# A linear-attention and gated feed-forward kernel: rows of x in another tile's place, loads and stores of x at other times, and another order of some splits

## The chip, the core and the metric

The kernel runs on one core of a Trainium2 chip. Its time is the device time of one execution in microseconds (us); the smaller, the better. The core has TensorE (PE; its weight loads are listed as PEld), VectorE (DVE), ScalarE (ACT), GpSimd (POOL) and SyncE (SP), which here issues every DMA.

## What is computed

For x of 2048 rows and 576 columns, in float32:

```
xn  = layernorm(x)
q,k,v = xn @ wqkv              (32 heads of 18 columns)
pq, pk = phi(q), phi(k)        phi(t) = (t > 0 ? t + 1 : exp(t)) + 1e-6
kv, z = sum over rows of pk v, sum over rows of pk      (per head)
s   = (pq kv) / (pq z + 1e-6) @ wo
g   = silu( gelu(xn @ w1 + b1) @ w2 + b2 )              (576 -> 4608 -> 576)
out = x + s * g
```

## The kernel before

Every float32 product is made of three: an operand is written as a rounded part `h` and a remainder `l`, both in the type fp32r, and TensorE adds h·h, h·l and l·h in PSUM. Making the two is a *split*: a copy to fp32r (`hi`, mostly on ScalarE, line 656) and a subtraction (`lo`, mostly on VectorE, line 659). SBUF tiles of xn, transposed, are `xh0`..`xh3` (five tiles of 128 rows by 512 columns each; 576 = 4·128 + 64, and the last 64 rows stand twice, once as `h` and once as `l`) and `xl0`..`xl3` (four each), one pair for every 512 rows of x, in the pool `xp`.

**Phase 1** (to about 166 us) runs over 16 tiles of 128 rows of x. Tile t loads x (`load_x`), takes mean and variance (`layernorm`, line 175 on), normalises, transposes on TensorE into PSUM (`transpose_x`, line 206), copies to `xh` and subtracts for `xl`, multiplies by the weights of k and v (`project`, line 229: 14 matmul pairs into one PSUM tile) and adds up the state. The loads run ahead: x of tile t+3 is issued in tile t. Each weight of k is five pieces, `wk_h` and `wk_l`, split at the start. Along the way other things are prepared: W2's sums (`w2r`), the last rows of w1 (`we`), the splits of wq (loaded in tiles 11 to 13), and xh0, xl0 and parts of xh1, xl1 are written to the DRAM tensor `x_dram` (after tiles 4 and 8), since their places are used for other things and the second half of the feed-forward needs them again.

All DMAs are in SP's one queue, in program order; a DMA on SP also waits for the one eight before it.

**The query phase** (to about 285 us) finishes the attention. It also makes the operands that the feed-forward's seven-product scheme wants: sums of blocks of x, and the last 64 rows of each of the seven products (`rest`), split and written to `rq_dram`.

**The feed-forward** (300 to 1082 us) treats the rows of x in two halves, and each half in nine chunks of 512 hidden columns, 18 chunks in all; a tail follows the last, whose down product is a plain one. So 17 chunks are alike. A chunk has 28 steps. Steps 0 to 13 are two `Up` objects: each makes a 2 by 2 block product with seven products instead of eight, in the order 1, 6, 7, 5, 2, 3, 4 (`Up.step`). Its PSUM tiles are `a`, `b`, `e` and `zy`; three intermediate sums, `m1`, `u1`, `u2`, stand in SBUF, in the tile `mid`. VectorE makes `b<-e,mid` (line 996), `e<-e,mid` (1003) and `zy<-zy,mid` (1007), and ScalarE makes a gelu `g` of each result (978). The products take xh, xl and the `rest` tile `rx` of their number as moving operands (`mm`). Steps 14 to 27 are the seven down products (`product`, line 1100) in the order 1, 2, 7, 4, 5, 3, 6, each in two calls (two of four quarters of 128 rows at a time). Product 2 adds to what product 1 left in its PSUM tile, 3 to that of 5 and 4 to that of 7 (`CHAIN`); before that, VectorE adds the tile of 1, 5 or 7 into the accumulator `macc` (line 1107), and TensorE waits for this.

The operands of the down products are the gelu results and their sums: POOL makes the sums in place, `S` (5,.) at line 1060, (6,.) at 1063, (3,.) at 1066 and (7,.) at 1069, where (i, pr) is the product and which of the two `Up`s. Each operand is split by `hi` (ScalarE, 656) and `lo` (VectorE, 659). At which step of the chunk each of them is put in program order is written out by hand in the table `PH`, and `in_order` holds VectorE, ScalarE, POOL and TensorE to the program's order. The lines of `PH` for `lo` are

```
            (1, 0): 10, (2, 0): 10, (7, 0): 11, (1, 1): 12, (2, 1): 13, (7, 1): 15, (4, 0): 16,
            (4, 1): 17, (5, 1): 18, (5, 0): 19, (6, 0): 20, (3, 0): 21, (3, 1): 22, (6, 1): 23,
```

Step 11 is the one in which the second `Up` makes its product 2, 12 is its product 3 (`e`), 13 its product 4 (`zy`). So VectorE's order at the end of the second `Up` is lo(1,0), lo(2,0), lo(7,0), e, lo(1,1), zy, lo(2,1), macc of product 1, ...

Memory: `mid` has the place of `xh1` in the pool `xp` (five tiles of 128 by 512; three for m1, u1, u2 and two for the operands of product 7). The rows `rest` of the products 5, 2, 3, 4 have four tiles of 128 by 512 in the pool `rx`, loaded by `load_rests` from `rq_dram`, two DMAs each; those of the other products are loaded elsewhere.

Of the kernel before, what the change touches and what calls it, by code (L numbers as in the profile page):

```python
# [8 lines left out]
F32 = mybir.dt.float32  # L9
# [6 lines left out]
P = 128  # L16
# [6 lines left out]
NT = S // P  # L23
# [19 lines left out]
def linear_attention_gated_ffn(ctx, tc, x, wqkv, wo, w1, w1e, b1, w2, b2, out):  # L43
# [121 lines left out]
    def load_x(t):  # L165
        xraw[t] = (
            stw.tile([P, D], F32, tag="stw", name=f"x{t}") if t < 2 else stage(D, f"x{t}")
        )
        nc.sync.dma_start(xraw[t], x[t * P : (t + 1) * P, :])

    xn, stats = {}, {}

    def layernorm(t):
        st = t1.tile([P, 2, 6], F32, tag="st", name=f"st{t}")
        nc.vector.bn_stats(st[:, 0, :], xraw[t][:, :HD])
        nc.vector.bn_stats(st[:, 1, :], xraw[t][:, HD:])
        mv = t1.tile([P, 4], F32, tag="mv", name=f"mv{t}")
        nc.vector.bn_aggr(mv[:, 0:2], st)
        nc.vector.tensor_scalar_add(mv[:, 2:3], mv[:, 1:2], 1e-5)
        nc.gpsimd.tensor_tensor(mv[:, 3:4], mv[:, 2:3], nhalf, op=ALU.pow)  # L180
        stats[t] = mv
        if t < 2:
            xn[t] = t1.tile([P, 640], F32, tag="xn", name=f"xn{t}")
            for dst, src in norm_parts(t):
                nc.vector.tensor_scalar(dst, src, mv[:, 0:1], mv[:, 3:4], op0=SUB, op1=MUL)
# [17 lines left out]
    def transpose_x(t):  # L203
        pt = bank2(f"pt{t}").rearrange("p a b -> p (a b)")
        for k in range(KT):
            nc.tensor.transpose(pt[:, k * P : (k + 1) * P], xn[t][:, k * P : (k + 1) * P], ident)  # L206
        b, c = divmod(t, 4)
        cs = slice(c * P, (c + 1) * P)
        p3 = pt[:, : KT * P].rearrange("p (k c) -> p k c", k=KT)
        if t == 0:  # L210
            nc.vector.tensor_copy(xh[b][:, :2, cs], p3[:, :2])
            nc.vector.tensor_copy(xh[b][:, 2:, cs], p3[:, 2:])
        else:
            nc.scalar.copy(xh[b][:, :, cs], p3)
        nc.vector.tensor_tensor(xl[b][:, :, cs], p3[:, :4, :], xh[b][:, :4, cs].bitcast(F32), op=SUB)
        nc.vector.tensor_tensor(
            xh[b][64:, 4, cs], p3[64:, 4, :], xh[b][64:, 4, cs].bitcast(F32), op=SUB
        )

    def project(t, hi, lo, ps):  # L220
        b, c = divmod(t, 4)
        cs = slice(c * P, (c + 1) * P)
        seq = []
        for k in range(4):
            seq += [(xh[b][:, k, cs], hi, k), (xh[b][:, k, cs], lo, k), (xl[b][:, k, cs], hi, k)]
        seq += [(xh[b][:, 4, cs], hi, 4), (xh[b][:, 4, cs], lo, 4)]
        for i, (st, w, k) in enumerate(seq):
            for h in range(2):
                nc.tensor.matmul(  # L229
                    ps[:, h, :HD], st, w[:, k, h * HD : (h + 1) * HD],  # L230
                    start=(i == 0), stop=(i == len(seq) - 1),
                )
# [11 lines left out]
    def load_w_raw(which, k):  # L244
# [4 lines left out]
        nc.sync.dma_start(raw, wqkv[k, :, which * D : (which + 1) * D])  # L249
        return raw  # L250

    def split_w(raw, k, hi, lo, elo):
        nc.scalar.copy(hi[:, k, :], raw)
        elo.tensor_tensor(lo[:, k, :], raw, hi[:, k, :].bitcast(F32), op=SUB)


    warm = bank1("warm")
# [158 lines left out]
    load_x(0)  # L416
    raw_k = [load_w_raw(1, k) for k in range(KT)]
    load_x(1)
    layernorm(0)
    split_w(raw_k[0], 0, wk_h, wk_l, nc.vector)  # L420
    split_w(raw_k[1], 1, wk_h, wk_l, nc.gpsimd)
    transpose_x(0)
    split_w(raw_k[2], 2, wk_h, wk_l, nc.gpsimd)
    split_w(raw_k[3], 3, wk_h, wk_l, nc.vector)
    split_w(raw_k[4], 4, wk_h, wk_l, nc.gpsimd)
    raw_v = [load_w_raw(2, k) for k in range(KT)]
    load_x(2)
    layernorm(1)
    pend = None
    WQ_LOADS = {11: (0,), 12: (1, 2), 13: (3, 4)}  # L430
    WQ_SPLITS = {13: (0,), 14: (1, 2), 15: (3, 4)}
    raw_q = {}
    for t in range(NT):
        if t + 3 < NT:
            load_x(t + 3)
        if t == 1:
            we_load(0), we_load(1)
        if 0 < t < NT - 2:
            layernorm(t + 2)
        pk = bank2(f"pk{t}")  # L440
        project(t, wk_h, wk_l, pk)
        if t == 0:
            for k in range(KT):
                split_w(raw_v[k], k, wv_h, wv_l, nc.vector)
        if t + 1 < NT:
            if t + 1 in (8, 12):
                x_block((t + 1) // 4)
            transpose_x(t + 1)
        for j in W2_SUMS.get(t - 1, ()):
            w2_hi(j)  # L450
        for j in W2_SUMS.get(t - 1, ()):
            w2_lo(j)
        if 2 <= t < 2 + WG:
            we_hi(t - 2), we_lo(t - 2)
        if t == 0:
            layernorm(2)
        if t + 2 < NT:
            offset(t + 2)
        k_t, _ = phi(t1, pk, f"k{t}")
        if pend is not None:  # L460
            state(*pend)
        pv = bank2(f"pv{t}")
        project(t, wv_h, wv_l, pv)
        v_t = t1.tile([P, D], F32, tag="v", name=f"v{t}")
        nc.scalar.copy(as2(v_t), pv[:, :, :HD])  # L465
        if t + 2 < NT:
            normalize_x(t + 2)
        if t == 0:
            nc.gpsimd.memset(zacc, 0.0)
        for j in W2_SUMS.get(t, ()):  # L470
            w2_sum(j)
        if 1 <= t < 1 + WG:
            we_sums(t - 1)
        nc.gpsimd.tensor_tensor(zacc, zacc, k_t, op=ADD)
        for k in WQ_SPLITS.get(t, ()):
            split_w(raw_q[k], k, wq_h, wq_l, nc.gpsimd if k == 0 else nc.vector)
        for k in WQ_LOADS.get(t, ()):
            raw_q[k] = load_w_raw(0, k)
        for j in W2_SUMS.get(t - 1, ()):
            w2_store(j)  # L480
        if 2 <= t < 2 + WG:
            we_store(t - 2)
            if t < WG:
                we_load(t)
        for c in W2_LOADS.get(t, ()):
            w2_load(c)
        if t == KT + 2:
            make_mask()
            nc.gpsimd.memset(kvz, 0.0)
        pend = (t, k_t, v_t)  # L490
        if t in (4, 8):
            b = t // 4 - 1
            if b == 0:
                nc.sync.dma_start(x_dram[:, 0:4], xh[0][:, :4].bitcast(F32))
                nc.sync.dma_start(x_dram[:, 4:8], xl[0].bitcast(F32))
            else:
                nc.sync.dma_start(x_dram[:, 10:12], xh[1][:, 2:4].bitcast(F32))
                nc.sync.dma_start(x_dram[:, 14:16], xl[1][:, 2:].bitcast(F32))
    nc.sync.dma_start(b1c, b1)
    query(0)  # L500
    state(*pend)
# [425 lines left out]


    gp = ctx.enter_context(tc.tile_pool(name="gp", bufs=1, side="right", reuse_waits="tile"))
    rx = ctx.enter_context(tc.tile_pool(name="rx", bufs=1, side="right", reuse_waits="tile"))  # L930
    gg = ctx.enter_context(tc.tile_pool(name="gg", bufs=NGT, side="right", reuse_waits="tile"))
    fr = ctx.enter_context(tc.tile_pool(name="fr", bufs=1, side="right", reuse_waits="tile"))
    fl = ctx.enter_context(tc.tile_pool(name="fl", bufs=1, reuse_waits="tile"))
# [4 lines left out]
    nc.sync.dma_start(b2b, bass.AP(tensor=b2.tensor, offset=b2.offset, ap=[[0, P], [1, D]]))  # L938
    BIAS = {2: 0, 7: 1, 3: 1, 4: 0}

    def load_rests(half, some):

        out = {}
        for i in some:
            out[i] = rx.tile([P, 512], F32R, tag=f"rx{i}", name=f"rx{i}")
            load_rest(half, i, out[i])
        return out

    mid = xp.tile([P, KT, 512], F32R, tag="xh1", name="mid").bitcast(F32)
    m1_sb, u1_sb, u2_sb = (mid[:, i, :] for i in range(3))  # L950

    class Up:

# [88 lines left out]
    class HOps:  # L1042
# [11 lines left out]
        def S(self, i, pr):  # L1054
            A = lambda r, c: self.A[pr, r, c]
            tt = nc.gpsimd.tensor_tensor
            src = self.src
            if i == 5:
                src[5, pr] = A(1, 0)
                tt(src[5, pr], A(1, 0), A(1, 1), op=ADD)  # L1060
            elif i == 6:
                src[6, pr] = A(0, 0)
                tt(src[6, pr], src[5, pr], A(0, 0), op=SUB)  # L1063
            elif i == 3:
                src[3, pr] = A(0, 1)
                tt(src[3, pr], A(0, 1), src[6, pr], op=SUB)  # L1066
            else:
                src[7, pr] = mid[:, 3 + pr, :]
                tt(src[7, pr], A(0, 0), A(1, 0), op=SUB)  # L1069

        def hi(self, i, pr):
# [202 lines left out]
    def plan_w1(add, w, base, T, hi, lo):  # L1274
        for table, what in ((T, w.T), (hi, w.hi), (lo, w.lo)):
# [23 lines left out]
            (4, 1): 17, (5, 1): 18, (5, 0): 19, (6, 0): 20, (3, 0): 21, (3, 1): 22, (6, 1): 23,  # L1299
        },  # L1300
        lo={
            (1, 0): 10, (2, 0): 10, (7, 0): 11, (1, 1): 12, (2, 1): 13, (7, 1): 15, (4, 0): 16,
            (4, 1): 17, (5, 1): 18, (5, 0): 19, (6, 0): 20, (3, 0): 21, (3, 1): 22, (6, 1): 23,
        },
    )
# [14 lines left out]
    w2t[0].load_raw()  # L1320
    z = xsum[1]
    s2, s1, s4 = z.tiles
    xs = x_operands(z.h0, z.l0, z.h1, z.l1, s1, s2, s4, load_rests(1, (5, 2, 3, 4)))
    seq = ExitStack()
    seq.enter_context(in_order(nc.vector.engine, nc.scalar.engine, nc.gpsimd.engine, nc.tensor.engine))
    n_chunks = 2 * NC
    for step in range(n_chunks):
# [36 lines left out]
        if not plain:  # L1364
            if half == 0 and c == NC - 1:
                for k, at in X_AT.items():
                    add(base + at, load_x_part, k)
                add(base + 14, lambda: x_new.update(rs=load_rests(0, (5, 2, 3, 4))))
                add(base + 25, silu_first, C11)
                for k in range(2):  # L1370
                    add(base + 26 + k, combine, C12, nc.vector, slice(2 * k, 2 * k + 2))
# [95 lines left out]
```

## Time and profile before

| | us |
|---|---|
| three runs | 1115.74, 1117.62, 1121.1 |
| median | 1117.62 |
| profiled execution, its own time | 1114.33 |
| its span, first to last instruction | 1112.6 |
| TensorE busy | 1100.2 |
| VectorE busy | 806.6 |
| POOL busy | 455.1 |
| ScalarE busy | 454.8 |

The granted clock of TensorE was 1.000 over the whole span. The profile is of one execution. A row of a timeline is: start in us from the span's start, duration, engine, line of the kernel, operation, the tile written and those read (names without their numbers), how many instructions lie in the row, and in brackets how long the engine was idle before it and for whom. A row of waits has the time lost, how often, and the longest. A row of the page's fifth part has the number of instructions, the busy time of all in us, and the mean in ns, then the idle time before them. A busy matmul engine is not necessarily one at its peak: the matmuls are pipelined, and a usual 288-column matmul of a down product follows the one before after 0.133 us.

### The profile page before, as it was taken

To read this page: it belongs to the slowest core of one execution; us is meant where nothing else is said; L and a number is where in the kernel's file an instruction comes from. 1 tells how busy PE (TensorE), PEld (TensorE's weight loads), DVE (VectorE), ACT (ScalarE), POOL (GpSimd) and SP (SyncE) were. 2 spreads that over 40 slices of the span, in tenths; PEclk is the share of its full clock that TensorE was granted. 3 is DMA by queue.
4 is the path that set the end of the run, shared out by engine and by line. 5 is a ranking of instruction groups with operands and counts; after the bars stand their busy time and mean duration, and the time that the engine had idled before them with its cause. 6 is when DMAs were issued, how large, how long until landed. Compare 5 with 4: busy or idle time off the path is not lost.

```text
span 1112.6 us, 18603 instructions
## 1 busy us (share of the span) xinstructions
PE 1100.2 (99%) x6972; PEld 1018.2 (92%) x6972; DVE 806.6 (72%) x1159; ACT 454.8 (41%) x771; POOL 455.1 (41%) x392
## 2 busy tenths in 40 slices
PE   8989999999999999999999999999999999999998
PEld 8989998999998988989989899898898998989987
DVE  7667547999687887878878878666485574764866
ACT  4544444333544354453543544524233242242342
POOL 4966533333353463444524534325234142241340
PEclk9999999999999999999999999999999999999999
DMA  8698642364879568586595779997777677776552
GB/s 316 254 367 325 246 155 52 117 248 165 262 273 342 178 235 293 196 301 218 184 348 179 257 264 356 323 348 253 244 247 220 199 239 216 237 219 213 136 182 85
DMA packets 84968, 264.03 MB, mean 237 GB/s; under 512 B 10381, under 2 KB 20877, under 8 KB 81295
## 3 DMA queue, kind: packets, MB, share of 16 engines
q1 hardware_dynamic: 84879, 262.85, 69.3%
q8 instruction: 55, 0.90, 0.3%
q14 instruction: 34, 0.28, 0.1%
HBM read 166.69 MB, written 94.18 MB: 234 GB/s over the span
## 4 chain that ended last, share of the span: by engine, by line
PE 94%; DVE 2%; DMA 2%; POOL 1%; issue 1%; ACT 0%; SPq 0%; DVEq 0%; ACTq 0%
PE pm L1100 34%; PE a L970 10%; PE e L970 10%; PE zy L970 10%; PE b L970 5%; PE pq L229 5%; PE ps_s L632 5%; PE pv L229 4%; PE pk L229 4%; PE pd L1220 2%; DMA x<-x 1%; PE ps_kva L266 1%; PE ptp L614 1%; PE pt L206 1%; PE ps_kw L560 1%
## 5 line engine op out<-in xcount | busy, mean ns | idle before, releaser
L1107 DVE TENSOR_TENSOR macc<-pm,macc 128x576 f32<-128x576 f32 x218 | 164.3, 754 | 58.9 <-PE pm L1100 57.1
L656 ACT CAST h_h<-g 128x512 fp32r<-128x512 f32 x204 | 120.9, 620 | 136.0 <-PE pm L1100 134.8
L659 DVE TENSOR_TENSOR h_l<-g,h_h 128x512 fp32r<-128x512 f32 x204 | 164.8, 815 | 0.0
L1069 POOL TENSOR_TENSOR mid<-g 128x512 f32<-128x512 f32 x34 | 43.9, 1292 | 119.5 <-ACT g L978 119.5
L1063 POOL TENSOR_TENSOR g<-g 128x512 f32<-128x512 f32 x34 | 55.0, 1619 | 57.8 <-DVE h_l L659 56.4
L978 ACT ACTIVATE g<-b,b1c 128x512 f32<-128x512 f32 x36 | 24.8, 689 | 116.5 <-DVE b L996 116.5
L987 ACT COPY mid<-a 128x512 f32<-128x512 f32 x36 | 21.1, 587 | 117.4 <-PE a L970 117.4
L700 POOL TENSOR_TENSOR w1raw<-w1raw 128x256 f32<-128x256 f32 x18 | 16.9, 938 | 124.1 <-DVE wa L716 124.1
L1195 POOL TENSOR_TENSOR fin1l<-fin1h,fin1l 128x288 f32<-128x288 f32 x8 | 6.5, 809 | 129.8 <-DMA fin1l<-s_dram 71.9
L990 DVE TENSOR_TENSOR mid<-b,mid 128x512 f32<-128x512 f32 x36 | 24.7, 686 | 44.9 <-PE b L970 43.2
L1066 POOL TENSOR_TENSOR g<-g 128x512 f32<-128x512 f32 x34 | 55.4, 1629 | 2.7
L970 PE MATMUL a<-h0r,wa 128*128 128x512 f32 x144 | 50.6, 391 | 0.0
L970 PE MATMUL a<-xh,wa 128*128 128x512 f32 x144 | 50.6, 391 | 0.0
L1060 POOL TENSOR_TENSOR g<-g 128x512 f32<-128x512 f32 x34 | 46.7, 1373 | 2.7
L996 DVE TENSOR_TENSOR b<-e,mid 128x512 f32<-128x512 f32 x36 | 25.2, 699 | 30.5 <-PE e L970 30.5
L659 DVE TENSOR_TENSOR h_l<-mid,h_h 128x512 fp32r<-128x512 f32 x34 | 45.8, 1347 | 1.2
L597 POOL TENSOR_TENSOR pbuf<-phiq,den 128x576 f32<-128x576 f32 x16 | 20.4, 1277 | 63.6 <-DVE den L596 44.8
L993 DVE TENSOR_TENSOR mid<-zy,mid 128x512 f32<-128x512 f32 x36 | 24.9, 691 | 25.5 <-PE zy L970 25.5
L298 POOL TENSOR_TENSOR w2r<-w2r 128x576 f32<-128x576 f32 x27 | 40.5, 1506 | 5.1 <-DMA w2r<-w 4.4
L1003 DVE TENSOR_TENSOR e<-e,mid 128x512 f32<-128x512 f32 x36 | 24.9, 690 | 20.2 <-PE e L970 20.2
L978 ACT ACTIVATE g<-e,b1c 128x512 f32<-128x512 f32 x36 | 24.9, 691 | 32.8 <-DVE e L1003 32.8
L229 PE MATMUL pk<-wk_h,xh 128*128 128x288 f32 x160 | 34.5, 297 | 1.5 <-ACT v L465 0.8
(810 smaller groups left out, 3607.6 us busy)
## 6 DMA issues: line engine op xcount, KB each, us to landing
we<-we_dram SPq DMA_DIRECT2D x72, 224.0 KB
op<-w2o SPq DMA_DIRECT2D x27, 576.0 KB
w2raw<-w SPq DMA_DIRECT2D x10, 1152.0 KB
w2r<-w SPq DMA_DIRECT2D x9, 1152.0 KB
w1raw<-w SPq DMA_DIRECT2D x18, 512.0 KB
op_a<-wa SPq DMA_DIRECT2D x18, 512.0 KB
op_c<-wc SPq DMA_DIRECT2D x18, 512.0 KB
op_d<-wd SPq DMA_DIRECT2D x18, 512.0 KB
```

The lines of the kernel that those rows point to most:

```text
L229: nc.tensor.matmul(ps[:, h, :HD], st, w[:, k, h * HD : (h + 1) * HD], start=(i == 0), stop=(i == len(seq) - 1),)
L632: nc.tensor.matmul(ps[:, h, :HD], st[:, k, :], w[:, k, h * HD : (h + 1) * HD], start=(i == 0), stop=(i == len(seq) - 1),)
L656: nc.scalar.copy(pair[0], src)
L659: eng.tensor_tensor(pair[1], src, pair[0].bitcast(F32), op=SUB)
L970: nc.tensor.matmul(ps, st, mv, start=first and n == 0, stop=n == len(seq) - 1, skip_group_check=True,)
L978: nc.scalar.activation(g, ps, AF.Gelu_apprx_tanh, bias=b1c[:, f : f + 1])
L1060: tt(src[5, pr], A(1, 0), A(1, 1), op=ADD)
L1063: tt(src[6, pr], src[5, pr], A(0, 0), op=SUB)
L1066: tt(src[3, pr], A(0, 1), src[6, pr], op=SUB)
L1069: tt(src[7, pr], A(0, 0), A(1, 0), op=SUB)
L1100: nc.tensor.matmul(ps[:, q, :HD], hs[p][st][:, cs], m[:, p, :], start=(n == 0 and i not in CHAIN), stop=(n == len(seq) - 1), skip_group_ch ...
L1107: nc.vector.tensor_tensor(dst, src, dst, op=ADD)
```

## The change

1. A tile `rxm` takes the place `xh1` in the pool `xp`, and its slices hold the `rest` rows of the products 5, 2, 3 and 4; the pool `rx` is gone. The tile `mid` moves to a pool of its own, `md`, on the right side. On SP, the first of its eight loads stand ahead of the last writes of `s_dram` and `rq_dram`, where all eight followed parts of them before.
2. In tile 0, x of tiles 3 and 4 are loaded, and in tile t after it that of tile t+4.
3. The stores of x to `x_dram`, after tiles 4 and 8, are after tiles 11, 12, 13 and 14, one each.
4. The first splits: wk_l0 is made between the statistics of tile 0 and its normalisation; one of VectorE's two copies of the first transposes goes to ScalarE, and the subtraction of xl0 is in two parts; wk_l3 and wk_l4 are both made by VectorE (wk_l4 by POOL before), between the statistics of tile 1 and its normalisation; and the first `project` takes its 14 pieces in another order, `FIRST`.
5. In `PH`, lo(1,1) is at step 11 (12 before) and lo(7,0) at step 14 (11 before). VectorE's order becomes lo(1,0), lo(2,0), lo(1,1), e, zy, lo(2,1), macc of product 1 (first half), lo(7,0), macc of product 1 (second half), lo(7,1), ...

The numbers of instructions of each engine stay, but for one more on VectorE and ScalarE and one fewer on POOL.

```diff
-    def layernorm(t):
+    def layernorm(t, between=lambda: None):
...
         nc.gpsimd.tensor_tensor(mv[:, 3:4], mv[:, 2:3], nhalf, op=ALU.pow)
         stats[t] = mv
+        between()
         if t < 2:
...
         if t == 0:
             nc.vector.tensor_copy(xh[b][:, :2, cs], p3[:, :2])
-            nc.vector.tensor_copy(xh[b][:, 2:, cs], p3[:, 2:])
+            nc.scalar.copy(xh[b][:, 2:, cs], p3[:, 2:])
         else:
             nc.scalar.copy(xh[b][:, :, cs], p3)
-        nc.vector.tensor_tensor(xl[b][:, :, cs], p3[:, :4, :], xh[b][:, :4, cs].bitcast(F32), op=SUB)
+        for k in (slice(0, 2), slice(2, 4)) if t == 0 else (slice(0, 4),):
+            nc.vector.tensor_tensor(xl[b][:, k, cs], p3[:, k], xh[b][:, k, cs].bitcast(F32), op=SUB)
...
+    PARTS = [p + str(k) for k in range(KT) for p in ("hh", "hl", "lh") if (p, k) != ("lh", KT - 1)]
+    FIRST = "hh0 hh1 lh0 lh1 hl0 hh2 lh2 hl1 hh3 lh3 hl2 hh4 hl3 hl4".split()
...
-    def project(t, hi, lo, ps):
+    def project(t, hi, lo, ps, order=PARTS):
...
-        seq = []
-        for k in range(4):
-            seq += [(xh[b][:, k, cs], hi, k), (xh[b][:, k, cs], lo, k), (xl[b][:, k, cs], hi, k)]
-        seq += [(xh[b][:, 4, cs], hi, 4), (xh[b][:, 4, cs], lo, 4)]
+        seq = [
+            ((xh, xl)[p[0] == "l"][b][:, int(p[2]), cs], (hi, lo)[p[1] == "l"], int(p[2]))
+            for p in order
+        ]
...
-    layernorm(0)
-    split_w(raw_k[0], 0, wk_h, wk_l, nc.vector)
+    layernorm(0, lambda: split_w(raw_k[0], 0, wk_h, wk_l, nc.vector))
     split_w(raw_k[1], 1, wk_h, wk_l, nc.gpsimd)
     transpose_x(0)
     split_w(raw_k[2], 2, wk_h, wk_l, nc.gpsimd)
-    split_w(raw_k[3], 3, wk_h, wk_l, nc.vector)
-    split_w(raw_k[4], 4, wk_h, wk_l, nc.gpsimd)
+    for k in (3, 4):
+        w_hi(raw_k[k], k, wk_h)
+
+    def last_lo():
+        for k in (3, 4):
+            w_lo(raw_k[k], k, wk_h, wk_l, nc.vector)
+
...
-    layernorm(1)
+    layernorm(1, last_lo)
...
+    X_STORES = {
+        11: lambda: (0, xh[0][:, :4]), 12: lambda: (4, xl[0]),
+        13: lambda: (10, xh[1][:, 2:4]), 14: lambda: (14, xl[1][:, 2:]),
+    }
     raw_q = {}
     for t in range(NT):
-        if t + 3 < NT:
-            load_x(t + 3)
+        for n in (3, 4) if t == 0 else (t + 4,):
+            if n < NT:
+                load_x(n)
...
-        project(t, wk_h, wk_l, pk)
+        project(t, wk_h, wk_l, pk, PARTS if t else FIRST)
...
-        if t in (4, 8):
-            b = t // 4 - 1
-            if b == 0:
-                nc.sync.dma_start(x_dram[:, 0:4], xh[0][:, :4].bitcast(F32))
-                nc.sync.dma_start(x_dram[:, 4:8], xl[0].bitcast(F32))
-            else:
-                nc.sync.dma_start(x_dram[:, 10:12], xh[1][:, 2:4].bitcast(F32))
-                nc.sync.dma_start(x_dram[:, 14:16], xl[1][:, 2:].bitcast(F32))
+        if t in X_STORES:
+            at, src = X_STORES[t]()
+            nc.sync.dma_start(x_dram[:, at : at + src.shape[1]], src.bitcast(F32))
...
-    rx = ctx.enter_context(tc.tile_pool(name="rx", bufs=1, side="right", reuse_waits="tile"))
+    md = ctx.enter_context(tc.tile_pool(name="md", bufs=1, side="right", reuse_waits="tile"))
...
-    def load_rests(half, some):
-
+
+    rxm = xp.tile([P, KT, 512], F32R, tag="xh1", name="rxm")
+
+    def load_rests(half):
         out = {}
-        for i in some:
-            out[i] = rx.tile([P, 512], F32R, tag=f"rx{i}", name=f"rx{i}")
+        for k, i in enumerate((5, 2, 3, 4)):
+            out[i] = rxm[:, k]
             load_rest(half, i, out[i])
         return out
 
-    mid = xp.tile([P, KT, 512], F32R, tag="xh1", name="mid").bitcast(F32)
-    m1_sb, u1_sb, u2_sb = (mid[:, i, :] for i in range(3))
+    mid = md.tile([P, 5, 512], F32, name="mid")
+    m1_sb, u1_sb, u2_sb = (mid[:, i] for i in range(3))
...
-                src[7, pr] = mid[:, 3 + pr, :]
+                src[7, pr] = mid[:, 3 + pr]
...
         lo={
-            (1, 0): 10, (2, 0): 10, (7, 0): 11, (1, 1): 12, (2, 1): 13, (7, 1): 15, (4, 0): 16,
+            (1, 0): 10, (2, 0): 10, (1, 1): 11, (2, 1): 13, (7, 0): 14, (7, 1): 15, (4, 0): 16,
```

(In the calls of `load_rests` the second argument goes.)

More of the change, by code (lines that the diff above doesn't have):

```diff
@@ L218, in transpose_x @@
         )
-    def project(t, hi, lo, ps):
+    PARTS = [p + str(k) for k in range(KT) for p in ("hh", "hl", "lh") if (p, k) != ("lh", KT - 1)]
+    FIRST = "hh0 hh1 lh0 lh1 hl0 hh2 lh2 hl1 hh3 lh3 hl2 hh4 hl3 hl4".split()
+    assert sorted(PARTS) == sorted(FIRST)
+    def project(t, hi, lo, ps, order=PARTS):
         b, c = divmod(t, 4)
         cs = slice(c * P, (c + 1) * P)
-        seq = []
-        for k in range(4):
-            seq += [(xh[b][:, k, cs], hi, k), (xh[b][:, k, cs], lo, k), (xl[b][:, k, cs], hi, k)]
-        seq += [(xh[b][:, 4, cs], hi, 4), (xh[b][:, 4, cs], lo, 4)]
+        seq = [
+            ((xh, xl)[p[0] == "l"][b][:, int(p[2]), cs], (hi, lo)[p[1] == "l"], int(p[2]))
+            for p in order
+        ]
         for i, (st, w, k) in enumerate(seq):
@@ L250, in load_w_raw, with w_hi, w_lo @@
         return raw
+    def w_hi(raw, k, hi):
+        nc.scalar.copy(hi[:, k, :], raw)
+    def w_lo(raw, k, hi, lo, elo):
+        elo.tensor_tensor(lo[:, k, :], raw, hi[:, k, :].bitcast(F32), op=SUB)
     def split_w(raw, k, hi, lo, elo):
-        nc.scalar.copy(hi[:, k, :], raw)
-        elo.tensor_tensor(lo[:, k, :], raw, hi[:, k, :].bitcast(F32), op=SUB)
+        w_hi(raw, k, hi)
+        w_lo(raw, k, hi, lo, elo)
     warm = bank1("warm")
@@ L1322, in linear_attention_gated_ffn @@
     s2, s1, s4 = z.tiles
-    xs = x_operands(z.h0, z.l0, z.h1, z.l1, s1, s2, s4, load_rests(1, (5, 2, 3, 4)))
+    xs = x_operands(z.h0, z.l0, z.h1, z.l1, s1, s2, s4, load_rests(1))
     seq = ExitStack()
@@ L1367, in linear_attention_gated_ffn @@
                     add(base + at, load_x_part, k)
-                add(base + 14, lambda: x_new.update(rs=load_rests(0, (5, 2, 3, 4))))
+                add(base + 14, lambda: x_new.update(rs=load_rests(0)))
                 add(base + 25, silu_first, C11)
```

## The prediction

> **What bounds the kernel now.** I read the page's first part, then the engines' waits, then the timeline of every stage in which the change has an edit.
>
> ```profile
> PE 1100.2 (99%) x6972; PEld 1018.2 (92%) x6972; DVE 806.6 (72%) x1159; ACT 454.8 (41%) x771; POOL 455.1 (41%) x392
> ```
>
> TensorE is the bound: 1100.2 of 1112.6 us. No edit takes a matmul away, so a gain can only come out of its gaps, and a loss is a new gap. The waits, by line (us, count, longest):
>
> ```profile
> PE pt L206 <- ACT xn L201: 2.2, 1, 2.2
> PE pk L229 <- ACT v L465: 0.8, 1, 0.8
> ```
>
> Both are one event in phase 1. VectorE stood for x of tile 7, and the transposes after it came late:
>
> ```profile
> 71.61 0.46 DVE L175 BATCH_NORM_STATS2 st<-x 128x6 f32<-128x288 f32 x1 [6.52 <-DMA x<-x]
> 79.51 0.77 PE L206 MATMUL pt<-ident,xn 128*128 128x128 f32 x5 [2.22 <-ACT xn L201]
> ```
>
> The chain of waits has that load too: issued at 59.46, 12.13 us to landing. The chunks of the feed-forward come next (the one whose products start near 406, as a sample). The timeline of VectorE, then POOL, ScalarE, TensorE:
>
> ```profile
> 402.35 1.28 DVE L659 TENSOR_TENSOR h_l<-g,h_h 128x512 fp32r<-128x512 f32 x2
> 403.71 1.63 DVE L659 TENSOR_TENSOR h_l<-mid,h_h 128x512 fp32r<-128x512 f32 x1
> 405.26 0.69 DVE L1003 TENSOR_TENSOR e<-e,mid 128x512 f32<-128x512 f32 x1
> 405.86 1.18 DVE L659 TENSOR_TENSOR h_l<-g,h_h 128x512 fp32r<-128x512 f32 x1
> 407.56 0.68 DVE L659 TENSOR_TENSOR h_l<-g,h_h 128x512 fp32r<-128x512 f32 x1
> 408.32 0.76 DVE L1107 TENSOR_TENSOR macc<-pm,macc 128x576 f32<-128x576 f32 x1
> ...
> 403.17 1.61 POOL L1063 TENSOR_TENSOR g<-g 128x512 f32<-128x512 f32 x1 [3.05 <-DVE h_l L659]
> 404.86 1.63 POOL L1066 TENSOR_TENSOR g<-g 128x512 f32<-128x512 f32 x1
> 409.82 1.30 POOL L1060 TENSOR_TENSOR g<-g 128x512 f32<-128x512 f32 x1
> 404.29 0.62 ACT L656 CAST h_h<-g 128x512 fp32r<-128x512 f32 x1
> ...
> 407.10 0.40 PE L1100 MATMUL pm<-w__4593,h_l 128*128 128x288 f32 x1
> 409.72 0.43 PE L1100 MATMUL pm<-w__4612,h_h 128*128 128x288 f32 x2
> ```
>
> The reader is to see: the splits `lo` (L659) in order are (1,0) and (2,0), (7,0), (1,1), (2,1). (2,1) takes 0.68. (7,0) takes 1.63 and ends at 405.34, 0.55 after POOL's L1063 ended (404.78); (1,1) takes 1.18 and ends at 407.04, 0.55 after L1066 ended (406.49). So a split, which reads two SBUF operands, does nothing while a POOL operation runs. The reverse too: L1063 and L1066 took 1.6, begun under a split, against 1.30. The additions from PSUM (`e`, 0.69; `macc`, 0.76) don't stretch. TensorE's row at 407.10 needs lo(1,1): the gap around it is 0.16 us in each of the 17 chunks with products, the only gap there.
>
> **The change, part by part.**
>
> *x a tile sooner, stores later.* The load of x7 stood behind 1 MB stores of xh and xl, W2 and w1 loads; the queue was full (DMA share 1.00 and 1.04 in the 9 us windows from 45 and 54). A tile takes 9.05 us, so issuing one tile sooner covers the 6.52 us stand, and the first two stores leave this stretch. Gain 2.22 + 0.78 = 3.0 us. Bounds: 0 if it only moves, 3.0 as there is no more. What could be late next is what the stores now meet at tiles 11 to 14: 3.15 MB at the 380 GB/s of the full windows is 8.3 us, and the windows from 117 to 153 have shares of 0.66, 0.69, 0.52, 0.37, which leaves 15.8 us. Loads issued there are used 7 us and more later (W2 at 129.19 for 141, wo up to 159.3 for 166.2). SP runs in order and each of its DMAs waits for the one eight before it; a 1 MB store cost it 1.22 us at 57.65, so four cost some 5 us of SP over 36. At the start one x load passes W2's first, which is used tiles later. I take 3.0.
>
> *First splits.* TensorE's first projection ran from 7.70 to 12.7, its last piece waiting for wk_l4 on POOL (three splits, 4.71 us for the group, ending 12.10); the next transposes start at 13.29 after a 0.60 wait for xn1. Now wk_l0 goes ahead of xn0 (0.75 us, but xn0 waits for POOL's power meanwhile: pt0 about 0.2 later), ScalarE takes one of VectorE's copies (its split of wk_h1 goes first), the splits of 3 and 4 are VectorE's, and the first matmuls take pieces in order of readiness. With 0.7 to 1.7 for each of the two splits (1.71 is wk_l3's row under POOL), the projection ends near 12.35 and pt1 starts near 12.5. Gain 0.8; bounds -0.2 (xn1 behind both splits) and 1.5 (all of the waits).
>
> *Rests in `rxm`, sums in `md`.* Same instructions, other addresses. SP issues the first four rests before the split's writes instead of after; two wait there for these writes to land. Before, they cost SP 2.96 and 3.11 us and the last group was issued 3.6 us before TensorE's use at 303.31, with no gap. If a group comes late by its whole issue time the loss is 3.1 once; nothing is late by the rows, so 0.
>
> *The order of `lo` in each chunk*: (1,1) one step sooner, (7,0) three later. (1,1) is what the 0.16 gap waits for, but it meets POOL. Before, (7,0) was queued when L1063 ended, and VectorE had the port first; L1066 was begun under it. After, nothing of VectorE is queued at 404.78: lo(1,1) waits for ScalarE's cast, which ends at 404.91, and can start at 404.94, 80 ns after L1066 (404.86). Where POOL began 82 to 89 ns before a split (L705 at 416.91 against the split at 416.99) the split waited in 8 of 8 chunks. So L1066 now runs alone, 404.86 to 406.16, and lo(1,1) ends 0.55 later, at 406.71. TensorE needs it at about 406.95: that gap goes. But `e` stands behind it on VectorE:
> - `e` starts at 406.63, not 405.26: 1.37 later. ScalarE's gelu of it, the cast of (2,1) and lo(2,1) follow on, so lo(2,1) runs 408.73 to 409.41 (before 407.56 to 408.24).
> - the first `macc` is next: 409.33 to 410.08 (before 408.32 to 409.08). Product 2 adds into that PSUM tile, so TensorE waits for it; it wants to start at 409.58 (409.72 less the gap gone). It starts near 410.23, with the 0.06 from lo(1,1)'s end (407.04) to the row at 407.10, and the 0.10 by which that row's first matmul is longer than the usual 0.133: 0.65 lost.
> - lo(7,0) comes after, now under POOL's L1069: 1.15. The second `macc` ends at 411.83, where product 2's second half loses 0.16. The following splits stretch like those before (1.08 to 1.12), and the first `macc` of product 7 is late for product 4 by 0.31. Then VectorE has caught up.
>
> Sum 1.12 a chunk in place of 0.16: 0.96 x 17 = +16.4 us. Bounds: -0.16 a chunk (-2.7) if (1,1) gets the port first; +1.21 (+20.6), the full 1.37 less 0.16. I take the walk, because the row nearest to the race, 82 to 89 ns, has one outcome.
>
> The Trainium skill speaks against this term: "Advanced Engine Details and Errata", Mode Summary, says that the port shared with GpSimd makes 2-port Vector instructions and GpSimd's block each other; by its letter a tensor_tensor, not in that table's modes, would run past POOL, and the sum would be 1107.8. "SBUF — State Buffer", Who interferes with whom, has a tensor_tensor with two SBUF inputs contend, and lets the one that starts first keep the pair. The rows of 1.18 and 1.63 against 0.68 bear out the second.
>
> **Sum:** 1114.33 (the profiled execution: span 1112.6, 1.73 around it) - 3.0 - 0.8 + 16.4 = 1126.9. The three runs shown have a median 3.3 above that execution, the lowest 1.4 above. I give 1128.5, half of that difference added.
>
> **Rivals.**
> *A: lo(1,1) first.* At 404.86 to 404.94 VectorE takes the port before L1066, runs 0.68, and L1066 moves behind it. Then `e` is at 405.54, `macc` is in time, and the 0.16 goes: 1114.33 - 3.0 - 0.8 - 2.7 = 1107.8, up to 1111 with the offset: faster. It decides at a shift of 80 ns between ScalarE's cast and POOL. The same time comes if the split just runs beside L1066; the stretched rows leave 0.02 of A's chance to that. For A: where VectorE began 80 to 90 ns ahead of a POOL operation (L703) it won 8 of 8, so a small shift suffices. Against: both starts hang on rows that the change leaves alone.
> *B: the order costs nothing.* Lateness of 1.0 at `macc` is taken up, and the gap only moves: 1110.5, with the offset 1111 to 1114. Against: `macc` had 0.64 us to spare, and the walk overruns it.
> *C: the x stand only moves.* The stores delay what comes at tiles 12 to 15, the order as forecast: 1129.9. Against: the 15.8 us of room.
>
> **How the numbers follow.** 0.68 for the forecast, C within it; its own range is 1118 (0.4 a chunk, only the first late `macc`, halved) to 1133 (1.21 a chunk and the offset). A 0.22, B 0.10. Half a per cent, 5.6 us, is about what a measurement of this kernel can tell from no change. Of A three quarters lie below 1112, of B a quarter: faster 0.20. Slower is 0.66, the forecast less its low end; same 0.14. The range goes down into A, 1109 to 1133.
>
> **What would show it.** Right: TensorE has no gap at x7; pt1 starts near 12.5; in each chunk POOL's L1066 takes about 1.30, lo(1,1) ends some 0.55 after it, `e` starts 4.2 us after the addition into `b` ended, and product 2 starts after a wait on `macc`. Wrong: a lo(1,1) of 0.68 with L1066 longer (A), or a late `e` without a gap at product 2 (B). If the gap at 79.5 turns up at 125 to 165 instead, the stores moved it; a gap near 303 is the rests.

## The result, and the profile after

The changed kernel took 1126.84 us in the median of four runs (1125.94 to 1127.98), the kernel before 1117.34 (the three runs shown above and one more). The ratio is 1.0081, with a 95% interval of 1.0053 to 1.0108: slower by 9 us. The forecast was 1128.5, in 1109 to 1133. The profiled execution took 1125.94, with a span of 1124.2; the sum of the forecast for it was 1126.9.

The page's first part, of the changed kernel:

```profile
PE 1103.8 (98%) x6972; PEld 1018.5 (91%) x6972; DVE 795.4 (71%) x1160; ACT 452.4 (40%) x772; POOL 451.3 (40%) x391
```

TensorE's work is the same, 6972 matmuls; the span is 11.6 us longer. TensorE's waits, by line (us, count, longest):

```profile
PE pm L1119 <- DVE macc L1126: 7.8, 15, 0.6
...
PE pm L1119 <- DVE macc L1132: 1.0, 2, 0.5
PE pt L207 <- DVE xn L186: 0.7, 1, 0.7
```

15 + 2 waits for `macc` are the 17 chunks with products. The waits of 2.2 and 0.8 us at tile 8 are no longer there. The sample chunk of the changed kernel (its addition into `b` ends at 400.34; lines are 17 to 19 higher than before), first VectorE, POOL and ScalarE:

```profile
399.64 0.70 DVE L1015 TENSOR_TENSOR b<-e,mid 128x512 f32<-128x512 f32 x1 [0.90 <-PE e L989]
402.84 1.76 DVE L676 TENSOR_TENSOR h_l<-g,h_h 128x512 fp32r<-128x512 f32 x1 [1.32 <-ACT h_h L673]
404.53 0.69 DVE L1022 TENSOR_TENSOR e<-e,mid 128x512 f32<-128x512 f32 x1
406.62 0.69 DVE L676 TENSOR_TENSOR h_l<-g,h_h 128x512 fp32r<-128x512 f32 x1 [0.81 <-ACT h_h L673]
407.23 0.75 DVE L1126 TENSOR_TENSOR macc<-pm,macc 128x576 f32<-128x576 f32 x1
...
402.76 1.29 POOL L1085 TENSOR_TENSOR g<-g 128x512 f32<-128x512 f32 x1
...
402.19 0.62 ACT L673 CAST h_h<-g 128x512 fp32r<-128x512 f32 x1
405.25 0.69 ACT L997 ACTIVATE g<-e,b1c 128x512 f32<-128x512 f32 x1 [2.44 <-DVE e L1022]
```

Then TensorE at the second product:

```profile
407.25 0.29 PE L1119 MATMUL pm<-w__4591,h_l 128*128 128x288 f32 x1
408.04 0.54 PE L1119 MATMUL pm<-w__4610,h_h 128*128 128x288 f32 x2 [0.49 <-DVE macc L1126]
```

This is the chain that was forecast, row by row. The cast (402.19, 0.62) ends at 402.81, POOL's L1085 is under way since 402.76, and lo(1,1) begins at 402.84 and takes 1.76; it ends 0.55 after POOL does. So it goes in all 17 chunks: POOL's operation begins 81 to 86 ns ahead of lo(1,1) in the first ten and 138 to 143 ns ahead in the other seven, and lo(1,1) takes 1.70 to 1.76. `e` starts 4.19 us after the addition into `b`, ScalarE is idle for 2.44 waiting for it, lo(2,1) and the first `macc` follow, and TensorE stands between its products 1 and 2.

Along the span the two traces part like this (the same event in both, after less before): the first matmul of pv0 -0.29 us, the start of the feed-forward (its first matmul, at 293.94 before) -3.76, the end of the 17 chunks with products +11.3, the end +11.6. A chunk took 45.00 us before and 45.90 after, each of them within 0.02, but for the step to the last, plain one (45.62 and 46.52).

### The profile page after: what moved, and what is told of

It reads as the page before. It is cut to its first block, busy times and chain, and to the rows that moved or that the text cites. A ratio compares the mean times of both kernels' runs of the same rounds, so it can differ in the third digit from the quotient of the medians.

```text
span 1124.2 us, 18622 instructions
## 1 busy us (share of the span) xinstructions
PE 1103.8 (98%) x6972; PEld 1018.5 (91%) x6972; DVE 795.4 (71%) x1160; ACT 452.4 (40%) x772; POOL 451.3 (40%) x391
## 5 line engine op out<-in xcount | busy, mean ns | idle before, releaser
L676 DVE TENSOR_TENSOR h_l<-g,h_h 128x512 fp32r<-128x512 f32 x204 | 174.8, 864 | 37.0 <-ACT h_h L673 21.3
L1085 POOL TENSOR_TENSOR g<-g 128x512 f32<-128x512 f32 x34 | 49.7, 1461 | 2.7
L217 DVE TENSOR_TENSOR xl<-pt,xh 128x512 fp32r<-128x512 f32 (+1 forms) x17 | 11.1, 660 | 47.9 <-ACT xh L215 47.3
L676 DVE TENSOR_TENSOR h_l<-mid,h_h 128x512 fp32r<-128x512 f32 x34 | 38.6, 1134 | 0.0
```

The costliest lines, as they stand in the source:

```text
L676: eng.tensor_tensor(pair[1], src, pair[0].bitcast(F32), op=SUB)
```

## The experiments

The theory going in: the loss is the order of `lo` (theory 1), by way of POOL's operation and a late `e`. Every run below is compared with runs of the kernel before on the same chip: after the median stands the ratio to it, with its 95% interval. "Chunk" is the time from one chunk's addition into `b` to that of the next, away from the change of halves; before it is 45.00 us.

**The order of `lo` alone, and everything but it.** `lo_only` is the kernel before with the two entries of the table; `lo_back` is the changed kernel without them.

```diff
-            (1, 0): 10, (2, 0): 10, (7, 0): 11, (1, 1): 12, (2, 1): 13, (7, 1): 15, (4, 0): 16,
+            (1, 0): 10, (2, 0): 10, (1, 1): 11, (2, 1): 13, (7, 0): 14, (7, 1): 15, (4, 0): 16,
```

> The kernel before with the order of lo alone taken from the change. Theory 1 (the loss is the order of lo in the 17 chunks, through POOL's L1066 and a late e): TensorE waits for macc before product 2 by about 0.5 us in each chunk, the chunk's gaps add 1.10 us as in the changed kernel, 17 x 1.10 = 18.7, so 1114.3 + 18.7 = 1133 for a profiled run; slower than the change, whose other parts gain. Theory 2 (the loss comes from the places of rxm and mid, or from what the stores meet): no wait before product 2, 1112 (0.16 x 17 gained).

Measured: 1132.73 us, ratio 1.0152 [1.0134, 1.0170]; chunk 46.00. The chunk grew by 1.00, not 1.10; that the time still came to the 1133 expected is in part chance. In this trace the granted clock of TensorE fell to 0.5 from 80.00 to 83.42, behind the stop of 2.2 us for x of tile 7, which costs about 1.7 us (half of 3.4) once; the trace of the kernel before has the same stop without it.

> The changed kernel with the order of lo as before. Theory 1: the waits for macc are gone and the 0.16 us gap at the l-operand of product 1 is back; what is left of the change is 0.29 at the start, 3.47 at x and the 0.2 us a chunk by which the products of an Up came closer together: 1114.3 - 3.8 - 3.4 = 1107. Theory 2: the loss stays, 1124 to 1129.

Measured: 1108.95 us, 0.9943 [0.9923, 0.9963]; chunk 44.89. So the order of `lo` costs 1.00 to 1.01 us a chunk, with or without the rest, 17 us; everything else in the change, taken together, gains. The profiled execution of `lo_back` took 1112.26, since two of its chunks are 2.25 and 1.36 longer than the others (see the change of halves).

**Which of the two moves.** In `only_11` lo(7,0) is back at 11 with (1,1) behind it; in `only_70` (1,1) is back at 12, and (7,0) stays at 14; their lines stand in this order.

```diff
-            (1, 0): 10, (2, 0): 10, (1, 1): 11, (2, 1): 13, (7, 0): 14, (7, 1): 15, (4, 0): 16,
+            (1, 0): 10, (2, 0): 10, (7, 0): 11, (1, 1): 11, (2, 1): 13, (7, 1): 15, (4, 0): 16,
+            (1, 0): 10, (2, 0): 10, (1, 1): 12, (2, 1): 13, (7, 0): 14, (7, 1): 15, (4, 0): 16,
```

> The changed kernel with lo(7,0) back at step 11 and lo(1,1) behind it at step 11, ahead of e. Theory 1 (what costs is that e stands behind lo(1,1) while POOL has the port): e starts 4.5 us after the end of the addition into b, later still than in the change; product 2 waits about 0.8 longer than before, a chunk is 0.97 longer than the kernel before's by the walk: 1123 to 1126. Theory 3 (what costs is lo(7,0), put behind the first macc where L1069 blocks it): no wait before product 2 worth more than 0.2 us, 1105 to 1108.

Measured: 1126.86 us, 1.0099 [1.0079, 1.0119]; chunk 45.90, `e` 4.52 after the addition into `b`, 17 waits for `macc`, 10.1 us in all. This is 0.9 over the top of theory 1, and far from theory 3.

> The changed kernel with lo(1,1) back at step 12, behind e, and lo(7,0) left at step 14. Theory 1: e starts 2.5 us after the addition into b, lo(1,1) still waits for L1066 but ends at about 4.27, before TensorE needs it; no wait before product 2, no 0.16 us gap: 1107.2 - 2.7 = 1104.5. Theory 3: lo(7,0) still makes a macc late, 1112 to 1124.

Measured: 1107.06 us, 0.9918 [0.9892, 0.9944]; chunk 44.68. It is 2.6 over what was expected; in the trace, 1.6 of it lie in the chunk at the change of halves (below). VectorE of `only_70` (the addition into `b` ends at 397.82):

```profile
400.30 0.70 DVE L1022 TENSOR_TENSOR e<-e,mid 128x512 f32<-128x512 f32 x1 [1.28 <-PE e L989]
400.90 1.19 DVE L676 TENSOR_TENSOR h_l<-g,h_h 128x512 fp32r<-128x512 f32 x1
402.61 0.68 DVE L676 TENSOR_TENSOR h_l<-g,h_h 128x512 fp32r<-128x512 f32 x1
403.47 0.76 DVE L1126 TENSOR_TENSOR macc<-pm,macc 128x576 f32<-128x576 f32 x1 [0.18 <-PE pm L1119]
```

lo(1,1) is held up by POOL here too (1.19), but `e` is ahead of it, and the first `macc` now waits for TensorE instead of the other way round. What costs is putting lo(1,1) ahead of `e`, as long as POOL's operation holds lo(1,1) up there. Moving lo(7,0) away is worth 0.21 us a chunk by itself (44.89 to 44.68): it takes the old gap away.

**Is it POOL?** `s30_later` leaves every order of VectorE as in the change and moves one sum of POOL behind another. `s30_lo_back` does the same with the order of `lo` as before.

```diff
-        S={(7, 0): 7, (5, 0): 8, (6, 0): 11, (3, 0): 11, (7, 1): 13, (5, 1): 14, (6, 1): 15, (3, 1): 15},
+        S={(7, 0): 7, (5, 0): 8, (6, 0): 11, (7, 1): 13, (3, 0): 14, (5, 1): 14, (6, 1): 15, (3, 1): 15},
```

> The changed kernel with all orders of VectorE as in the change; only POOL's sum (3,0), L1085 here (L1066 before), is put after its sum (7,1) and so runs some 4.5 us later. Theory 1 (lo(1,1) waits for the POOL operation that began 80 ns ahead of it): lo(1,1) takes 0.68 us in place of 1.76, e starts 3.1 us after the addition into b in place of 4.2, product 2 starts without a wait; the moved sum may make a later macc or split late by 0.1 to 0.25 us a chunk. Chunk 44.7 to 45.0 us in place of 45.90: 1106 to 1112. Rival (the order of VectorE itself costs, whatever POOL does): the wait for macc stays, 1125 and more.

Measured: 1112.64 us, 0.9980 [0.9971, 0.9990]. In the sample chunk (`b` done at 399.33), VectorE:

```profile
401.83 0.69 DVE L676 TENSOR_TENSOR h_l<-g,h_h 128x512 fp32r<-128x512 f32 x1 [1.32 <-ACT h_h L673]
402.44 0.69 DVE L1022 TENSOR_TENSOR e<-e,mid 128x512 f32<-128x512 f32 x1
```

The same split at the same place in the same order takes 0.69 in place of 1.76, `e` starts 3.12 after the addition into `b`, and no product waits for the first `macc`. So nearly all of the loss needs POOL's operation; the order of VectorE without it does not make it. The chunk is 45.25 in the first half and 44.99 in the second, 0.25 over the top of what was expected in the first: POOL's later sums stretch (1.75 against 1.30) and hold up later splits, and TensorE has gaps of 0.14 to 0.24 at products further on. The profiled execution took 1116.88, 4.2 over the median: TensorE waited 1.9 us at the change of halves, and its granted clock was 0.5 twice, for 3.4 us each.

> The changed kernel with the order of lo as before, and POOL's sum (3,0) after (7,1). Theory 1: the gap that was there before (TensorE waits for lo(1,1), 0.24 us a chunk at the faster pace of the Ups) came from the same POOL operation, L1066 before: lo(1,1) falls from 1.18 to 0.68 us, the gap goes, chunk 44.67 in place of 44.89 us, 17 x 0.22 = 3.7 us under the kernel with the order of lo put back: 1105 to 1107. Rival (the gap comes from lo(1,1) standing behind lo(7,0) and e): the chunk stays at 44.89, 1109.

Measured: 1106.53 us, 0.9922 [0.9908, 0.9935]; chunk 44.65, lo(1,1) 0.68:

```profile
400.29 0.69 DVE L1022 TENSOR_TENSOR e<-e,mid 128x512 f32<-128x512 f32 x1
400.89 0.68 DVE L676 TENSOR_TENSOR h_l<-g,h_h 128x512 fp32r<-128x512 f32 x1
```

The 0.16 us gap of the kernel before came from the same operation of POOL. The Trainium skill, "SBUF — State Buffer", Who interferes with whom, says that a tensor_tensor with two SBUF inputs contends with GpSimd and that the order of issue decides who is blocked; these four kernels agree: 1.76 behind a POOL operation 80 ns ahead, 0.68 and 0.69 with none.

**The other parts alone.** The core of each edit to the kernel before, in the order `x_only` (with the stores at tiles 11 to 14), `first_only` (with the other lines of the first splits), `rxm_only` (with `rxm` in the place of xh1) and `pad_only`:

```diff
-        if t + 3 < NT:
-            load_x(t + 3)
+        for n in (3, 4) if t == 0 else (t + 4,):
+            if n < NT:
+                load_x(n)
...
-    layernorm(0)
+    layernorm(0, lambda: split_w(raw_k[0], 0, wk_h, wk_l, nc.vector))
...
-    mid = xp.tile([P, KT, 512], F32R, tag="xh1", name="mid").bitcast(F32)
+    mid = md.tile([P, 5, 512], F32, name="mid")
...
+    rx.tile([P, 512], F32R, tag="rxpad", name="rxpad")
```

> The kernel before with the loads of x one tile sooner and the four stores at tiles 11 to 14, nothing else. Theory 1 (each part adds up by itself): the stand at x7 and both of TensorE's gaps after it go, 3.47 us as in the trace of the change, no gap from 117 to 166: 1114.3 - 3.5 = 1110.8 for a profiled run. Rival: without the earlier rest loads and the shorter start the stand moves to another load, 0 to 2 us gained.

Measured: 1112.77 us, 0.9970 [0.9957, 0.9983]. TensorE's two gaps are gone and the feed-forward starts 3.60 us sooner; 3.3 us stay in the timed runs. In the profiled one, 2.7 of it were given back in three chunks at and behind the change of halves (below).

> The kernel before with the first splits in the order of the change, nothing else. Theory 1: the first matmul of pv0 starts at 13.52 in place of 13.81, 0.3 us, and all else moves with it: 1114.0, no difference that a timing shows. Rival (the forecast's 0.8 is there but is hidden by the earlier loads of x in the change): pt1 starts near 12.5, 0.8 us.

Measured: 1114.76 us, 0.9998 [0.9982, 1.0013]: nothing. pv0 started at 12.96 in this trace, 0.85 sooner than in the profile before. But with the old splits the six traces have it at 13.32 to 13.81 (mean 13.51), with the new ones the eight have 12.96 to 14.22 (mean 13.43). The 14.22 is not a matter of loads alone: in that trace (`s30_later`) the granted clock was 0.5 from 8.60 to 12.01. Without it the seven have 12.96 to 13.53 (mean 13.31), so a gain of some 0.2 is not excluded. Kernels with the same splits differ by half a microsecond with when the pieces of wk and x1 land: in the change, the statistics of x1 begin at 9.84, after 0.65 of waiting for its load, in `first_only` at 9.28.

> The kernel before with the tiles rxm and md in place of rx and mid, nothing else. Theory 1 (where the operands lie sets the pace of the matmuls in an Up): the mean from one 512-column matmul to the next falls from 229.2 ns to 227.2 in the feed-forward, 1764 of them, 3.5 us: 1110.8. Rival (the pace is a by-product of the changed order of lo, of TensorE's waits): 229.2 stays, 1114.3.

Measured: 1113.55 us, 0.9988 [0.9969, 1.0007]; chunk 44.89; from one matmul of an Up to the next 227.2 ns, before 229.1. The timed runs alone do not tell this from no change; the traces do, in every chunk away from the change of halves.

> The kernel before with one more, unused tile of 2 KB in the pool rx, so that the pools gg and fr lie 2 KB further on, as in the change, while rx and mid stay. If the pace of the Ups comes from the places of rx or mid it stays at 229.2 ns and the time at 1114.3; if it comes from the 2 KB by which gg and fr moved, it is 227.2 and 1110.8.

Measured: 1116.74 us, 0.9998 [0.9988, 1.0008]; 229.1 ns, chunk 45.00. The 2 KB are not it. `rx_left` moves only the pool `rx` to the other side:

```diff
-    rx = ctx.enter_context(tc.tile_pool(name="rx", bufs=1, side="right", reuse_waits="tile"))
+    rx = ctx.enter_context(tc.tile_pool(name="rx", bufs=1, reuse_waits="tile"))
```

> The kernel before with the pool rx on the left side of SBUF in place of the right one; mid stays in the place of xh1 and nothing else changes but that gg and fr lie 8 KB further back. It tells apart which of the two moved tiles sets the pace of the Ups. If it is the place of rx, the rest matmul of product 5 and the products 2, 3 and 4 go from some 231 ns a matmul to 226.7, 2 ns in the mean, as with rxm. If it is the place of mid (m1, u1, u2, written and read by ScalarE and VectorE meanwhile), the pace stays at 229.1. Time 1111 to 1114 either way, as TensorE's wait for lo(1,1) grows by part of what is gained.

Measured: 227.2 ns and chunk 44.89, as with `rxm`, and yet 1118.94 us, 1.0029 [1.0016, 1.0041]. So the pace comes from where the four `rx` tiles lie. It is not the place of `mid`. (`rx_left` also moves `gg` and `fr`, by 8 KB; but `rxm_only` has them 2 KB further on, where `pad_only` has them, and the one is fast and the other slow.) The mean time from a matmul to the next, in ns, for the seven matmuls of some products (the last one reads the rest tile), worked out from the traces:

```
              before                                        rx_left
product 7     227 227 227 227 227 227 227                   227 227 227 227 227 227 227
product 5     227 227 227 227 227 227 233                   227 227 227 227 227 227 227
product 2     226 236 228 233 231 227 233                   227 227 227 227 227 227 227
product 4     226 235 228 233 231 227 232                   227 227 227 227 227 227 226
```

Before, the slower pace starts at the first matmul that reads `rx` and goes on through the three products that use the others, also in their matmuls that read x (product 3 is as product 2). Product 1, which reads no `rx`, varies from 225 to 234 in all of these kernels. The time `rx_left` lost is in TensorE's waits and behind one of them. Its eight loads of `rx` were issued from 296.21 on, where four of them were issued at 274.53 before; the first use waited, and so did a product of a later chunk.

```profile
PE e L970 <- DMA rx<-rq_dram: 2.1, 1, 2.1
PE pm L1100 <- DVE h_l L659: 1.9, 1, 1.9
```

Behind the first of the two waits the granted clock was 0.5 from 303.14 to 306.56, some 1.7 us more; of 5.7 us lost, the pace (1.9) and an earlier start of the feed-forward (0.4) give 2.3 back, which leaves about the 3.3 by which the span is longer. In a table of windows the clock stands before the DMA share:

```profile
304.00:305.00 1.00, 1.00 (x4) 0.80 (x3) 0.61 (x1) 1.00 (x3) 0.00 (x0) 0.50 1.73 348
```

**The change of halves.** Most of the kernels that come there sooner have a gap that neither the kernel before nor the changed one has: `rxm_only` 0.7 us, `s30_lo_back` 1.3, `lo_back` 1.8, `s30_later` 1.9. (`x_only` is 3.6 sooner and has none; `only_11` comes later and has 0.2.) In `only_70`:

```profile
PE a L989 <- DMA wa<-op_a: 1.4, 1, 1.4
```

SP stands there on the eight loads of rests (14.05 us from 683.39 in that trace), and the loads of w1's operands come behind them. `half14` is `only_70` with these loads put first.

```diff
-            add(base + (16 if change else 14), load_we, 2 * step + 3)
+            add(base + 14, load_we, 2 * step + 3)
...
-            add(base + (16 if change else 14), make, W1Loaded, w1t, 2 * step + 3)
+            add(base + 14, make, W1Loaded, w1t, 2 * step + 3)
```

> The kernel with only lo(7,0) moved (lo(1,1) back at 12), and at the change of halves the loads of w1's operands for the second Up go to SP ahead of the eight loads of rests, on which SP stands for 14 us. If the wait of 1.4 us for wa at the first products of the second half (it shows only in the kernels that come to it 2 us and more earlier) is this place in SP's queue, it goes and nothing takes its place: 1104 to 1106. Rival: the DMA engines are full there, and the rests or x of the second half come late by as much: 1107.

Measured: 1113.43 us, 0.9979 [0.9967, 0.9992], slower than `only_70`: the rival, and by more than it said. The wait for wa is gone, and the rests came late; the DMA share of the windows from 690 to 700 is 1.02 to 1.05. TensorE's waits of `half14`, and SP:

```profile
PE e L989 <- DMA rxm<-rq_dram: 5.5, 1, 5.5
...
688.43 14.73 SPq L834 DMA_DIRECT2D rxm<-rq_dram  x8
```

The eight loads still take SP 14.7 us, from 5.0 us later on. Not all of the 7.7 us by which this chunk is longer than its neighbours is the wait: the granted clock was 0.5 from 701.11 to 707.93, in the last 2.5 us of it and for 4.3 us after it, which is some 2.1 more. Either order of the two leaves one of them late, so the loads of the change of halves, and not the chunks, are what a faster chunk meets next. Whether fewer bytes or fewer DMAs there would help was not tried.

Four traces (`lo_back`, `only_11`, `x_only`, `rx_left`) have a second gap there, of 1.2 to 1.9 us, two chunks later: a product waits for a split. In `lo_back` POOL stood 28.42 us for a load of finished output and was busy with its sums (lines 1214, 1215) until 758.57; its sums for the products come behind them, and lo(7,0) and lo(1,1) take 1.77 and 1.16 under these. `e`, behind lo(7,0), starts 4.20 after the addition into `b`, as late as in the change. The rows of the other three are alike. No run tests this.

## Why the prediction was right

By its own steps:

- *The order of `lo`*, +16.4 (0.96 a chunk; 17 times that is 16.3). Right, with its mechanism: `lo_only` gives 1.00 a chunk, 17.1. The forecast's times within the chunk held to 0.02 us: lo(1,1) ends 4.26 after the addition into `b` (4.27 forecast), `e` starts at 4.19 (4.19), lo(2,1) at 6.28 (6.29), the first `macc` ends at 7.64 (7.64). L1066, L1085 now, took 1.29. The 80 ns race fell as the rows of 82 to 89 ns said. TensorE's three stops in the chunk measured 0.76, 0.17 and 0.33 us with their refills, where the walk had 0.65, 0.16 and 0.31. The first is larger because the Ups ran faster (below), so TensorE stood at product 2 some 0.1 sooner.
- *x a tile sooner*, -3.0. Right, a little small: -3.47 between pv0 and the feed-forward. The sum took the idle time of the two rows, 2.22 and 0.78, and left out what TensorE loses around a stop, some 0.1 to 0.2 at each end. The stores fit: the windows from 117 to 153 rose to shares of 0.85, 1.00, 0.74 and 0.78, with TensorE busy in all of them.
- *First splits*, -0.8. Wrong: -0.29 in the trace, and by `first_only` nothing that a timing shows. The step that failed was to walk the start by operations alone. The start also hangs on when loads land, and it varies from trace to trace by more than the gain.
- *Rests in `rxm`*, 0. Wrong in kind, small in size: no rest came late, but the place made the Ups 0.19 us a chunk faster. Of this 0.08 went into a longer wait for lo(1,1) in `rxm_only`, and 0.11 stayed (45.00 to 44.89), 1.9 us over the 17 chunks. The step that failed is "same instructions, other addresses", and with it the premise that a gain can only come out of TensorE's gaps: here the matmuls themselves came closer together. The trace before had the sign of it, the 233 ns beside 227, but not that another place would remove it.

So +17.1 - 3.5 - 0.3 - 1.9 = +11.4 against 11.6 in the two profiles; the forecast's sum was +12.6, and in the medians it is 9.5. Two misses, 0.5 at the start and 1.9 at the pace, and two undersized terms (0.7 at the order, 0.5 at x) partly cancel, so that the number came this close is in part luck. The 1.6 added to the sum for the median was a little much: the median lies 0.9 above the profiled execution.

Rival A, lo(1,1) first, is excluded by the rows (POOL at 402.76, the split at 402.84 with 1.76). A itself was not run, so its 1107.8 stays open. Nearest to it is `s30_later`, where lo(1,1) goes first in 0.69 and `e` starts at 3.12 (3.10 in A), but POOL's sum comes later than it would in A: 1112.6. B, that the lateness is taken up, falls with the 17 waits. C falls with the windows, and with the feed-forward, which starts 3.76 sooner.

`only_70` and `s30_lo_back` each take 0.8% less than the kernel before, and can't be told apart by these runs. Both keep the change's other parts and have `e` ahead of lo(1,1) again; `only_70` leaves lo(7,0) at its later step, and `s30_lo_back` takes POOL out from in front of lo(1,1).

## What to carry to other kernels

Before an operation is put ahead of another on an in-order engine, look at what the neighbour engine starts in that moment: here 0.16 us of waiting was to be removed, and an SBUF split put 80 ns behind a POOL operation made the addition behind it, and all that hung on that, 1.4 us late. The better move was the one that put less ahead of the urgent operation (lo(7,0) later), not the one that put the late operand sooner. Removing stalls early can bring the kernel sooner to stretches where the DMA queue is full, as at the change of halves here, so a gain shown in one stage has to be looked for at the end of the span.

## What the runs showed of the hardware that was not expected

Where a matmul's moving operand lies in SBUF can change the pace: with the four `rx` tiles on the right side, the matmul after each that reads them came 232 to 233 ns behind it, and others in these products up to 236, where 227 is usual; with the same tiles on the left side, or in the place of xh1, these all came at 227. Why is open: the runs tell the place of `rx` from that of `mid` and from a shift of 2 KB, but not one address from another.

A stop of TensorE can cost more than its length. In four traces the granted clock fell to 0.5 during a stop or soon after it: in `lo_only` after 2.2 us of standing (3.4 us at 0.5), in `rx_left` after 2.1 (3.4), in `s30_later` after 1.3 and after 1.9 (3.4 each), in `half14` in a stop of 5.5 (6.8). In others it did not: the kernel before has the 2.2, `lo_back` one of 1.8, and the clock stayed at 1.000 behind them. What decides it is open.
